# Idle matmuls behind real ones in the waits of TensorE, in the last steps of a fused attention, rational and soft-MoE kernel

## The chip, the cores and the metric

The kernel runs on one core of a Trainium2 chip. The metric is the device time of one execution in microseconds (us); the time before is the median of three runs.

## The reference

All arithmetic is float32. Three stages follow one another on 3072 tokens of width 512:

```python
# 1. chunked attention, 32 queries against 8 memory and 56 context keys
a = softmax(scale * q_c @ k_full.T); out[chunk] = a @ v_full
# 2. rational feed-forward, d_ff = 2048
h = x @ w_in
g = (a0 + a1*h + a2*h2 + a3*h3) / (1 + |b0|*|h| + |b1|*h2 + 1e-6)
x = g @ w_out
# 3. soft mixture of experts: 8 experts of 4 slots, inner width 1024
logits = x @ phi                                  # 3072 x 32
slot_input = softmax(logits, axis=0).T @ x        # 32 x 512
slot_out[e] = relu(slot_input[e] @ w1[e]) @ w2[e]
return softmax(logits, axis=1) @ slot_out
```

## The kernel before

The tokens go in 6 blocks of 512. A block has 8 steps, one for each 256 columns of w_in, so there are 48 steps (k = 0 to 47). `h_part` (L336) makes h of one step in a PSUM tile `h` of two banks (two such tiles rotate). The rational of the step runs on ScalarE and VectorE (in `run_step`, L544) and leaves g, transposed, in an SBUF tile `T`. `post` (L349) then takes that tile on TensorE: it multiplies it by `wp` (w_out times phi, L361) into the logits `lg`, and transposes it (L368) for ScalarE to copy into a `g` tile (L369). Multiplying by w_out itself is put off to the end: `soft1` (L375) to `soft3` (L413) do the running softmax of a block over its logits and add the block's slot sums, `p_tok.T @ g` (L419), to `u_acc` (L424).

The last two steps have code of their own, `last_steps` (L600). The rational of step 46 goes over whole tiles (L624, L625), that of step 47 in two halves (L628 to L630). Between them step 45 is posted (L623). After the steps `post` of 46 and 47, `soft1`, `soft2` and `soft3` of the last block follow, then the end: `u_acc` is transposed (L668), multiplied by w_out (L675) and by the softmax's denominator (L680), which gives the slot inputs; they are transposed (L683), spread by expert (L687) and go through w1 (`first`, L690) and w2 (L733, L741). The last stage multiplies by the second softmax and writes the output (L765 to L773).

w_out, w1 and w2 of the end come in pieces of 512 KB, issued by `fill` (L513) on SyncE's DMA queue (SP) into any SBUF tile that has come free. `wants` lists them in the order of use. The queue is in order, so a piece that waits for its tile holds all later pieces. The eight pieces of `fill(p_g, "g", 4, 2)` (L659) take the four `g` tiles of the last block, which `soft3` reads.

The order of TensorE outside the end is set by the framework's scheduler. Only the instructions from L714 on (and those of the start) stand in the order in which they are written. An engine takes its instructions in order.

There is already a `busy(n)` (L281) in the start of the kernel: it issues n matmuls of the identity by itself into a PSUM tile that nobody reads. They are float32, and each shows in the trace as two matmul records.

Of the kernel before, what the change touches and what calls it, by code (L numbers as in the profile page):

```python
# [43 lines left out]
def tile_chunk_attention__rational__soft_moe(  # L44
# [15 lines left out]
    PE, ACT, DVE, POOL, SP = nc.tensor, nc.scalar, nc.vector, nc.gpsimd, nc.sync  # L60

    NPAIR, P, HP, _ = qw.shape
# [4 lines left out]
    NSLOT = 32  # L67
    NE, _, EFF = w1.shape
# [3 lines left out]
    BLK = 512  # L72
    NBLK = NT // BLK
# [29 lines left out]
    ps_h = Pool(ctx.enter_context(tc.tile_pool(name="ps_h", bufs=2, space=PSUM)))  # L103
# [3 lines left out]
    def bank(shape):  # L107
        return ps_m("m", shape)
# [4 lines left out]
    ident = const("ident", [P, P])  # L113
    stack = const("stack", [P, P])
    ctab = const("ctab", [P, 8])
    wp = const("wp", [P, NF, NSLOT])
    u_acc = const("u", [P, BLK])
# [138 lines left out]
    start = ExitStack()  # L256
# [90 lines left out]
    st = {}  # L347

    def post(k, part):  # L349

        b, i = divmod(k, NSTEP)
        qd, o = divmod(i, 2)
        t_ = gt_tile[k]
        if part == 0:
            if i == 0:
                st["lg"] = ps_l("lg", [P, BLK])
            if o == 0:
                gts[b, qd] = p_g("g", [P, TT, 4 * P])
            else:
                for j in range(4):  # L360
                    PE.matmul(st["lg"][32 * j:32 * j + 32, :], lhsT=wp[:, 4 * qd + j, :],  # L361
                              rhs=gt_tile[k - 1 + j // 2][:, j % 2, :],
                              start=(qd == 0), stop=(qd == NF // 4 - 1))
        pb = bank([P, 2, 2 * P])
        for m in range(2):
            for f2 in range(2):
                tt = 2 * part + m
                PE.transpose(pb[:, m, f2 * P:f2 * P + P], t_[:, f2, tt * P:tt * P + P], ident)  # L368
        ACT.activation(gts[b, qd][:, 2 * part:2 * part + 2, 2 * P * o:2 * P * o + 2 * P], pb, AF.Copy)  # L369
        if part and o:  # L370
            del gt_tile[k - 1], gt_tile[k]
# [3 lines left out]
    def soft1(b):  # L375
        lgs = p_s2("s2", [P, BLK])
        ACT.activation(lgs, st["lg"], AF.Copy)
        lt = bank([P, BLK])
        PE.matmul(lt, lhsT=stack, rhs=lgs, start=True, stop=True)
        ct = bank([P, TT, NSLOT])  # L380
        for tt in range(TT):
            PE.matmul(ct[:, tt, :], lhsT=lgs[:, tt * P:tt * P + P], rhs=stack[:, 0:NSLOT], start=True, stop=True)
        old, neg_m = (run[:, n:n + 1] for n in ((2, 0) if b % 2 else (0, 2)))
        bm, db = p_sm("bm", [P, 1]), p_sm("db", [P, 1])
        DVE.tensor_reduce(bm, lt, AX.X, ALU.max)
        if b == 0:
            DVE.tensor_scalar(neg_m, bm, -1.0, None, ALU.mult)
        else:
            DVE.tensor_scalar(neg_m, bm, -1.0, old, ALU.mult, ALU.min)
            ACT.activation(alpha, old, AF.Exp, bias=neg_m, scale=-1.0)  # L390
        pl = p_s2("s2", [P, BLK])
        ACT.activation(pl, lt, AF.Exp, bias=neg_m, accum_out=db)
        if b == 0:
            DVE.tensor_copy(den, db)
        else:
            DVE.tensor_scalar(den, den, alpha, db, ALU.mult, ALU.add)
        cm = p_sm("cm", [P, TT])
        ce = c_all[:, b, :].rearrange("p (t s) -> p t s", t=TT)
        DVE.tensor_reduce(cm, ct, AX.X, ALU.max)
        DVE.tensor_tensor(ce, ct, cm.unsqueeze(2).to_broadcast([P, TT, NSLOT]), ALU.subtract)  # L400
        ACT.activation(ce, ce, AF.Exp)
        DVE.tensor_reduce(csum[:, b * TT:b * TT + TT], ce, AX.X, ALU.add)
        st["pl"], st["ce"] = pl, ce
# [9 lines left out]
    def soft3(b):  # L413
        ce = st.pop("ce")
        p_tok = st.pop("ptok")
        pb = bank([P, BLK])
        for tt in range(TT):
            for j in range(4):
                PE.matmul(pb[32 * j:32 * j + 32, :], lhsT=p_tok[:, tt, :], rhs=gts[b, j][:, tt, :],  # L419
                          start=(tt == 0), stop=(tt == TT - 1))  # L420
        if b == 0:
            DVE.tensor_copy(u_acc, pb)
        else:
            DVE.scalar_tensor_tensor(u_acc, u_acc, alpha, pb, ALU.mult, ALU.add)  # L424
        for j in range(4):
            del gts[b, j]
        pb = bank([P, P])
        PE.transpose(pb, ce.rearrange("p t s -> p (t s)"), ident)
        ACT.activation(c_all[:, b, :], pb, AF.Copy)

    def wp_chunk(i):
# [37 lines left out]
    def convert(what):  # L469
        kind, n = what[0], int(what[1])  # L470
        if n < NSTEP:
            for _ in {"s": split_w, "n": narrow_w_out, "w": wp_chunk, "z": wp_sum, "i": load_w_in, "o": load_w_out}[kind](n) or ():
                pass
# [55 lines left out]
    def w_out_rows(ft):  # L529
        return got["o", ft // 2][:, ft % 2, :]  # L530
# [13 lines left out]
    def run_step(kk, what):  # L544
# [52 lines left out]
        elif b == 0 and what[0] in "snwzio" and len(what) == 2:  # L597
            convert(what[0] + str(min(i + int(what[1]), NSTEP)))

    def last_steps():  # L600
        k, z = total - 2, total - 1
        for what in "a1 h0 d1 p0 p1 t a2 h1".split():
            run_step(k, what)
        hh = hs.pop(z)
        s, t, y = p_S("S", [P, 2, BLK]), p_T("T", [P, 2, BLK]), p_S("S", [P, 2, BLK])
        w = p_S("S", [P, 2, BLK])
        t_, q_, w_ = late.pop(k)
        for n in range(2):
            o = slice(n, n + 1)
            ACT.activation(s[:, o], hh[:, o], AF.Abs, scale=b0)  # L610
            ACT.activation(y[:, o], hh[:, o], AF.Square, scale=rb1)
            ACT.activation(t[:, o], hh[:, o], AF.Identity, bias=a2, scale=a3)
            DVE.scalar_tensor_tensor(s[:, o], y[:, o], QC, s[:, o], ALU.add, ALU.add)
            POOL.tensor_tensor(y[:, o], q_[:, o], w_[:, o], ALU.mult)
            DVE.tensor_tensor(t[:, o], t[:, o], hh[:, o], ALU.mult)
            DVE.scalar_tensor_tensor(t[:, o], t[:, o], a1, hh[:, o], ALU.add, ALU.mult)
        for n in range(2):
            o = slice(n, n + 1)
            ACT.activation(w[:, o], s[:, o], AF.Ln, scale=2.0 ** -LN_SHIFT)
            ACT.activation(w[:, o], w[:, o], AF.Exp, bias=ex_b, scale=-1.0)  # L620
            if n == 0:
                for part in range(2):
                    post(k - 1, part)  # L623
        DVE.scalar_tensor_tensor(t_, t_, a0, w_, ALU.add, ALU.mult)  # L624
        DVE.scalar_tensor_tensor(t_, y, 2.0, t_, ALU.subtract, ALU.mult, reverse0=True)  # L625
        for n in range(2):
            o = slice(n, n + 1)
            DVE.tensor_tensor(s[:, o], s[:, o], w[:, o], ALU.mult)  # L628
            DVE.scalar_tensor_tensor(t[:, o], t[:, o], a0, w[:, o], ALU.add, ALU.mult)
            DVE.scalar_tensor_tensor(t[:, o], s[:, o], 2.0, t[:, o], ALU.subtract, ALU.mult, reverse0=True)  # L630
        gt_tile[k], gt_tile[z] = t_, t

    for kk in range(total + 4):
        b, i = divmod(kk, NSTEP)
# [30 lines left out]

    pb = bank([P, 4, P])
    for n in range(4):
        PE.transpose(pb[:, n, :], u_acc[:, n * P:n * P + P], ident)  # L668
    ut = p_s2("s2", [P, 4, P])
    ACT.activation(ut, pb, AF.Copy)  # L670
    pb = bank([P, DM])
    for n in range(4):
        for j in range(4):
            ft = 4 * j + n
            PE.matmul(pb[32 * j:32 * j + 32, :], lhsT=ut[:, n, 32 * j:32 * j + 32],  # L675
                      rhs=w_out_rows(ft),
                      start=(n == 0), stop=(n == 3))
    fill(p_v, "v", 1, 2)
    si = p_s2("s2", [P, DM])
    ACT.activation(si, pb, AF.Copy, scale=rden)  # L680
    pb = bank([P, NC, NSLOT])
# [46 lines left out]
    for eq in range(2):  # L728
        for n in range(8 - 2 * eq):
            if eq == 0 and n in (2, 3):  # L730
                turn(1, n - 2)
            for j in range(4):
                PE.matmul(so[32 * j:32 * j + 32, :], lhsT=hts[eq][:, n, 32 * j:32 * j + 32],  # L733
                          rhs=got[("2", 4 * eq + j, n // 2)][:, n % 2, :],
                          start=(eq == 0 and n == 0), stop=False)
    W = DM // 2
    for j in range(4):
        for n in range(2):
            for w in range(2):
                g = (j + 2 * n + w) % 4  # L740
                PE.matmul(so[32 * g:32 * g + 32, W * w:W * w + W], lhsT=hts[1][:, 6 + n, 32 * j:32 * j + 32],  # L741
                          rhs=got[("2", 4 + j, 3)][:, n, W * w:W * w + W],
                          start=False, stop=(j == 3))
# [4 lines left out]
    pb = [bank([P, W]) for _ in range(2)]  # L748
# [5 lines left out]
    for b in range(NBLK):  # L754
        for half in range(2):
            ob = p_win("win", [P, 2, DM])
            if half:
                pb = [bank([P, DM]) for _ in range(2)]
            else:
                both = ps_h("h", [P, 2, DM])  # L760
                pb = [both[:, m, :] for m in range(2)]
            for m in range(2):
                g = 32 * (2 * half + m)
                for w in range(2):
                    PE.matmul(pb[m][:, W * w:W * w + W], lhsT=c_all[g:g + 32, b, :], rhs=so4[g:g + 32, w, :],  # L765
                              start=True, stop=True)
            for m in range(2):
                n = TT * b + 2 * half + m
# [66 lines left out]
```

## Time and profile before

| | |
|---|---|
| runs shown | 596.45, 598.99, 599.82 us, median 598.99 |
| the profiled execution | 599.5 us, of which the span is 597.7 us |
| busy share of the span | TensorE 91%, its weight loads 66%, VectorE 75%, ScalarE 70%, GpSimd 20% |
| mean granted clock of TensorE | 0.962 |
| DMA | 97.42 MB, mean 163 GB/s |

The span runs from the first instruction to the last. The granted clock is the part of full speed that the throttle lets TensorE have: 1.00 is 2.4 GHz, 0.50 is 1.2 GHz, and a value between them means that the level changed within the stretch. The DMA share is the mean busy share of the 16 DMA engines. An idle time with a releaser names the instruction whose end let the waiting one go.

### The profile page before, as it was taken

The page shows a single profiled execution, that of the slowest core. Times are in us where ns is not written, and L with a number is a line of the kernel's source. Part 1 is how long each engine was busy: PE and PEld are TensorE (multiplying, and loading weights), DVE is VectorE, ACT ScalarE, POOL GpSimd, SP SyncE. Part 2 cuts the span into 40 slices and gives each one's busy share as a digit, 9 for nine tenths or more (in the row PEclk, how much of TensorE's full clock was granted, in tenths as well). Part 3 has the DMA queues.
Part 4 walks back from the last instruction along what each step waited for, and adds up shares of the span by engine and source line. Part 5 has one row for each costly group of instructions (what it writes and reads, how often), then busy time and mean ns, then how long its engine had stood idle before and what let it go on. Part 6 is the DMA issues. An engine that isn't in the chain of part 4 may idle for free.

```text
span 597.7 us, 13661 instructions
## 1 busy us (share of the span) xinstructions
PE 545.7 (91%) x5944; PEld 392.3 (66%) x5944; DVE 449.3 (75%) x563; ACT 417.9 (70%) x542; POOL 120.9 (20%) x64
## 2 busy tenths in 40 slices
PE   6789699889999999999999999999999999579981
PEld 5677576667767777677776677776778577236350
DVE  3878999966987988878889698896887868721041
ACT  1589989876877878778777778687787869520131
POOL 0001221211313133131322223131322233100000
PEclk9899899798999999999999999999999999789996
DMA  8898976320220222202121032210375424969948
GB/s 353 357 325 315 370 271 236 109 104 1 107 73 19 89 71 106 72 10 98 72 107 70 3 106 72 107 38 35 107 254 169 141 77 143 390 254 383 411 167 324
DMA packets 21372, 97.42 MB, mean 163 GB/s; under 512 B 2624, under 2 KB 2752, under 8 KB 16320
## 3 DMA queue, kind: packets, MB, share of 16 engines
q1 hardware_dynamic: 20160, 92.35, 41.7%
q0 software_dynamic: 1152, 4.19, 1.7%
q8 instruction: 47, 0.77, 0.5%
q14 instruction: 13, 0.11, 0.1%
HBM read 86.05 MB, written 10.49 MB: 162 GB/s over the span
## 4 chain that ended last, share of the span: by engine, by line
PE 59%; DVE 13%; ACT 12%; DMA 8%; issue 3%; POOL 2%; SPq 0%; ACTq 0%; DVEq 0%; POOLq 0%
PE h L342 30%; PE m L368 4%; PE m L419 4%; PE lg L361 4%; ACT S L561 3%; PE m L224 3%; ACT S L562 3%; ACT g L369 2%; PE m L445 2%; DMA g<-in_moe_w_in_dram 2%; DMA g<-in_moe_w_out_dram 2%; DVE T L573 2%; DMA win<-in_moe_w_dram 2%; DVE T L574 2%; DMA T<-in_moe_w_dram 2%
## 5 line engine op out<-in xcount | busy, mean ns | idle before, releaser
L342 PE MATMUL h<-xt,win 128*128 128x512 f32 x1152 | 294.6, 404 | 7.6 <-ACT win L325 5.3
L342 PEld LDWEIGHTS h<-xt,win 128*128 128x128 f32 x1152 | 212.3, 191 | 55.2 <-ACT win L325 6.7
L539 POOL TENSOR_TENSOR S<-S,S 128x1024 f32<-128x1024 f32 x46 | 112.0, 2435 | 300.1 <-DVE S L563 288.6
L561 ACT ACTIVATE S<-h,ctab 128x1024 f32<-128x1024 f32 x47 | 52.5, 1117 | 58.1 <-PE h L342 56.4
L563 DVE SCALAR_TENSOR_TENSOR S<-S,S 128x1024 f32<-128x1024 f32 x47 | 57.5, 1223 | 45.8 <-ACT S L562 45.6
L368 PEld LDWEIGHTS m<-ident,T 128*128 128x128 f32 x384 | 44.6, 145 | 33.4 <-issue 14.5
L573 DVE TENSOR_TENSOR T<-T,h 128x1024 f32<-128x1024 f32 x47 | 57.1, 1214 | 6.7 <-ACT T L564 6.7
L368 PE MATMUL m<-ident,T 128*128 128x128 f32 x384 | 54.6, 283 | 7.9 <-DVE T L625 6.0
L574 DVE SCALAR_TENSOR_TENSOR T<-T,ctab,h 128x1024 f32<-128x1024 f32 x47 | 59.8, 1272 | 0.7
L586 DVE SCALAR_TENSOR_TENSOR T<-T,ctab,S 128x1024 f32<-128x1024 f32 x46 | 58.6, 1274 | 0.0
L587 DVE SCALAR_TENSOR_TENSOR T<-S,T 128x1024 f32<-128x1024 f32 x46 | 56.2, 1221 | 2.7 <-DVE T L586 0.5
L564 ACT ACTIVATE T<-h,ctab 128x1024 f32<-128x1024 f32 x47 | 57.5, 1223 | 0.0
L369 ACT ACTIVATE g<-m 128x512 f32<-128x512 f32 x96 | 53.4, 602 | 3.7 <-PE m L368 3.6
L579 ACT ACTIVATE S<-S,ctab 128x1024 f32<-128x1024 f32 x47 | 54.4, 1158 | 0.8
L578 ACT ACTIVATE S<-S 128x1024 f32<-128x1024 f32 x47 | 50.5, 1074 | 5.1 <-DVE S L563 3.3
L562 ACT ACTIVATE S<-h,ctab 128x1024 f32<-128x1024 f32 x47 | 52.7, 1122 | 0.5 <-DVE T L586 0.5
L361 PE MATMUL lg<-T,wp 128*32 128x512 f32 x192 | 37.2, 620 | 0.7 <-DVE T L587 0.7
L186 ACT ACTIVATE a<-a 128x512 f32<-128x512 f32 x22 | 13.7, 635 | 19.6 <-DVE a L185 19.6
L419 PE MATMUL m<-g,s 128*32 128x512 f32 x192 | 23.5, 634 | 0.4 <-ACT s L411 0.4
L333 POOL DMA_DIRECT2D wo<-win x8 | 4.7, 588 | 88.3 <-DVE win L303 68.8
L248 DVE TENSOR_TENSOR xt<-m,xt 128x512 fp32r<-128x512 f32 x24 | 16.3, 687 | 7.4 <-ACT xt L247 7.3
L247 ACT ACTIVATE xt<-m 128x512 fp32r<-128x512 f32 x24 | 14.3, 605 | 9.2 <-PE m L243 9.2
(181 smaller groups left out, 645.0 us busy)
## 6 DMA issues: line engine op xcount, KB each, us to landing
win<-in_moe_w_dram SPq DMA_DIRECT2D x32, 512.0 KB, 5.5
k<-in_kw_dram SPq DMA_DIRECT2D x11, 1024.0 KB, 6.7
v<-in_vw_dram SPq DMA_DIRECT2D x11, 1024.0 KB, 5.0
g<-in_moe_w_in_dram SPq DMA_DIRECT2D x8, 1024.0 KB, 7.4
g<-in_moe_w_out_dram SPq DMA_DIRECT2D x8, 1024.0 KB, 9.5
out_dram<-win SPq DMA_DIRECT2D x12, 512.0 KB, 6.3
q<-in_qw_dram SPq DMA_DIRECT2D x11, 512.0 KB, 4.0
wo<-win POOLq DMA_DIRECT2D x8, 512.0 KB, 6.9
```

The costliest lines, as they stand in the source:

```text
L342: PE.matmul(tile_[:, f2, :], lhsT=ww[:, c, f2 * P:f2 * P + P], rhs=xx[:, c, :], start=(n == 0), stop=(n == 3 * NC - 1))
L361: PE.matmul(st["lg"][32 * j:32 * j + 32, :], lhsT=wp[:, 4 * qd + j, :], rhs=gt_tile[k - 1 + j // 2][:, j % 2, :], start=(qd == 0), stop=(q ...
L368: PE.transpose(pb[:, m, f2 * P:f2 * P + P], t_[:, f2, tt * P:tt * P + P], ident)
L369: ACT.activation(gts[b, qd][:, 2 * part:2 * part + 2, 2 * P * o:2 * P * o + 2 * P], pb, AF.Copy)
L539: POOL.tensor_tensor(out, q, w, ALU.mult)
L561: ACT.activation(s, hh, AF.Abs, scale=b0)
L562: ACT.activation(y, hh, AF.Square, scale=rb1)
L563: DVE.scalar_tensor_tensor(s, y, QC, s, ALU.add, ALU.add)
L564: ACT.activation(t, hh, AF.Identity, bias=a2, scale=a3)
L573: DVE.tensor_tensor(t, t, hh, ALU.mult)
L574: behind[kk] = DVE.scalar_tensor_tensor(t, t, a1, hh, ALU.add, ALU.mult).ins
L586: DVE.scalar_tensor_tensor(t, t, a0, w, ALU.add, ALU.mult)
```

## The change

A new helper `keep_busy(ins, n, rhs)` places n matmuls on TensorE behind the instruction `ins`. Each multiplies the identity by the identity, or by `rhs`, into the first 128 columns of a tile `h` of PSUM that nobody reads. The tile is taken once, at the first call. In all 31 matmuls are added: 12 and 7 behind the last transpose of step 45's `post` (the 7 read `w`, ScalarE's result of step 47's first half, so they can't start before it), 5 behind the logits' turn in `soft1` of the last block, 2 behind the last transpose of `soft3`, 2 behind the transposes of `u_acc`, 3 behind the product with w_out. Nothing is removed.

```diff
@@ post
-                PE.transpose(pb[:, m, f2 * P:f2 * P + P], t_[:, f2, tt * P:tt * P + P], ident)
+                st["turn"] = PE.transpose(pb[:, m, f2 * P:f2 * P + P], t_[:, f2, tt * P:tt * P + P], ident)
@@ soft1
         for tt in range(TT):
-            PE.matmul(ct[:, tt, :], lhsT=lgs[:, tt * P:tt * P + P], rhs=stack[:, 0:NSLOT], start=True, stop=True)
+            done = PE.matmul(ct[:, tt, :], lhsT=lgs[:, tt * P:tt * P + P], rhs=stack[:, 0:NSLOT], start=True, stop=True)
+        if b == NBLK - 1:
+            keep_busy(done.ins, 5)
@@ soft3
-        PE.transpose(pb, ce.rearrange("p t s -> p (t s)"), ident)
+        done = PE.transpose(pb, ce.rearrange("p t s -> p (t s)"), ident)
+        if b == NBLK - 1:
+            keep_busy(done.ins, 2)
@@ before last_steps
+    idle = {}
+
+    def keep_busy(ins, n, rhs=None):
+        if "t" not in idle:
+            idle["t"] = ps_h("h", [P, 2, BLK])
+        with tc.issue_after(ins):
+            for _ in range(n):
+                PE.matmul(idle["t"][:, 0, 0:P], lhsT=ident, rhs=ident if rhs is None else rhs, start=True, stop=True)
+
@@ last_steps
             if n == 0:
                 for part in range(2):
                     post(k - 1, part)
+                keep_busy(st["turn"].ins, 12)
+                keep_busy(st["turn"].ins, 7, w[:, 0, 0:P])
@@ the end
-        PE.transpose(pb[:, n, :], u_acc[:, n * P:n * P + P], ident)
+        done = PE.transpose(pb[:, n, :], u_acc[:, n * P:n * P + P], ident)
+    keep_busy(done.ins, 2)
...
-            PE.matmul(pb[32 * j:32 * j + 32, :], lhsT=ut[:, n, 32 * j:32 * j + 32],
-                      rhs=w_out_rows(ft),
-                      start=(n == 0), stop=(n == 3))
+            done = PE.matmul(pb[32 * j:32 * j + 32, :], lhsT=ut[:, n, 32 * j:32 * j + 32],
+                             rhs=w_out_rows(ft),
+                             start=(n == 0), stop=(n == 3))
+    keep_busy(done.ins, 3)
```

The order of TensorE's instructions from step 45's transposes to the logits' turn, before (T_5487, T_5549 and T_5602 are the rationals of steps 45, 46 and 47):

```order
L368 MATMUL m_5625<-ident_106,T_5487 128x128 x4
L368 MATMUL m_5631<-ident_106,T_5487 128x128 x4
L368 MATMUL m_5663<-ident_106,T_5549 128x128 x4
L368 MATMUL m_5669<-ident_106,T_5549 128x128 x4
L361 MATMUL lg_5395<-T_5549,wp_109 32x512 x2
L361 MATMUL lg_5395<-T_5602,wp_109 32x512
```

and with the change, where line numbers are those of the changed file (h_5637 is the tile of the idle matmuls, S_5604 is `w`):

```order
L368 MATMUL m_5625<-ident_106,T_5487 128x128 x4
L368 MATMUL m_5631<-ident_106,T_5487 128x128 x4
L611 MATMUL h_5637<-ident_106 128x128 x12
L611 MATMUL h_5637<-S_5604,ident_106 128x128 x7
L368 MATMUL m_5683<-ident_106,T_5549 128x128 x4
L368 MATMUL m_5689<-ident_106,T_5549 128x128 x4
L361 MATMUL lg_5395<-T_5549,wp_109 32x512 x2
L361 MATMUL lg_5395<-T_5602,wp_109 32x512
```

The 19 stand between the transposes of step 45 and those of step 46, and no real instruction has changed places.

The order of TensorE's instructions around `soft3`'s last transpose and the transposes of `u_acc`, with the change:

```order
L430 MATMUL m_5762<-ident_106,call_113 128x128
L611 MATMUL h_5637<-ident_106 128x128 x2
L683 MATMUL m_5804<-ident_106,u_110 128x128 x4
L611 MATMUL h_5637<-ident_106 128x128 x2
L691 MATMUL m_5813<-x_5119,s_13_5811 32x512
```

Here, too, the idle ones are all that is new; before, L428, L668 and L675 followed one another. The 5 and the 3 stand likewise, between L382 and L409 and between L675 and L683. On the other engines and on the DMA queues the order is the same as before.

## Rows read from the trace of the kernel before

**Rows 1.** The chain that ended last: start us, us, what.

```profile
524.52 0.83 PE m L382 x8
...
526.83 0.45 PE m L409 x4
...
527.68 5.46 PE m L419 x32
...
533.17 0.76 DVE u L424
...
533.97 0.67 PE m L668 x4
...
535.37 3.69 PE m L675 x32
...
539.87 1.09 PE m L683 x8
...
562.72 10.12 DMA T<-in_moe_w_dram
```

**Rows 2.** SyncE's issues and what its queue waited for, 500 to 598 us.

```profile
533.03 3.78 SPq L526 DMA_DIRECT2D g<-in_moe_w_dram  x8
...
SPq L526 <- PE m L428: 9.4, 1, 9.4
```

**Rows 3.** Stretches: busy time by engine (instructions), granted clock, DMA share, GB/s.

```profile
514.00:515.00 1.00, 0.00 (x0) 0.00 (x0) 1.00 (x2) 1.00 (x4) 0.19 (x1) 1.00 1.01 414
515.00:516.00 1.00, 0.00 (x0) 0.00 (x0) 0.89 (x2) 0.97 (x3) 0.00 (x0) 0.60 1.03 418
...
521.00:522.00 1.00, 1.00 (x3) 0.18 (x2) 0.00 (x0) 0.00 (x0) 0.00 (x0) 0.50 1.07 426
522.00:523.00 1.00, 1.00 (x5) 0.37 (x4) 0.00 (x0) 0.26 (x1) 0.00 (x0) 0.99 1.01 401
...
528.00:529.00 1.00, 1.00 (x12) 0.26 (x8) 0.00 (x0) 0.00 (x0) 0.00 (x0) 0.93 0.90 360
529.00:530.00 1.00, 1.00 (x10) 0.24 (x6) 0.00 (x0) 0.00 (x0) 0.00 (x0) 0.50 0.16 66
...
532.00:533.00 1.00, 1.00 (x9) 0.05 (x1) 0.00 (x0) 0.00 (x0) 0.00 (x0) 0.87 0.00 0
...
534.00:535.00 1.00, 0.63 (x4) 0.39 (x4) 0.00 (x0) 0.28 (x1) 0.00 (x0) 1.00 0.95 111
...
565.00:570.00 5.00, 5.00 (x52) 1.56 (x48) 0.00 (x0) 0.00 (x0) 0.00 (x0) 1.00 1.03 409
```

**Rows 4.** TensorE in order of time: start us, us, line, tiles, count [idle before].

```profile
509.86 1.09 PE L368 MATMUL m<-ident,T 128*128 128x128 f32 x8
516.96 1.94 PE L368 MATMUL m<-ident,T 128*128 128x128 f32 x8 [6.01 <-DVE T L625]
...
521.32 1.38 PE L361 MATMUL lg<-T,wp 128*32 128x512 f32 x2
522.63 0.88 PE L368 MATMUL m<-ident,T 128*128 128x128 f32 x6
523.39 1.12 PE L379 MATMUL m<-s,stack 128*128 128x512 f32 x2
```

**Rows 5.** VectorE and ScalarE in order of time, the same stretch.

```profile
515.59 1.23 DVE L625 SCALAR_TENSOR_TENSOR T<-S,T 128x1024 f32<-128x1024 f32 x1
...
520.11 0.69 DVE L630 SCALAR_TENSOR_TENSOR T<-S,T 128x512 f32<-128x512 f32 x1
...
513.33 0.72 ACT L620 ACTIVATE S<-S,ctab 128x512 f32<-128x512 f32 x1
...
522.74 0.60 ACT L377 ACTIVATE s<-lg 128x512 f32<-128x512 f32 x1 [3.20 <-PE lg L361]
```

**Rows 6.** TensorE in order of time, 0 to 32 us: the identity matmuls of the start.

```profile
1.36 4.63 PE L284 MATMUL lg<-ident 128*128 128x128 f32 x20 [1.36 <-POOL ctab L286]
...
29.41 1.06 PE L284 MATMUL lg<-ident 128*128 128x128 f32 x8
```

## Prediction of the time after the change

> **What bounds the kernel now.** I began with the chain that ended last [rows 1]. Read from its end, it is first a DMA: the last piece of the experts' weights, issued at 562.72 and landed 10.12 us later, and everything behind it waits for that piece. So the end of the kernel is set by the stream of weights, and the next question is what holds that stream up. The DMA column answers [rows 3]: late in the stream the engines are full (share 1.03, 409 GB/s), but from 529 to 534 they are all but idle (0.16 from 529 to 530, 0.00 from 532 to 533) and full again from 534 (0.95). The queue's own waits name the cause [rows 2]: it waits 9.4 us for TensorE's L428, and at 533.03 eight pieces go out into the `g` tiles that `soft3` has just read. The stream thus starts again when L419 is done, and from there it runs full to the end. A microsecond won on TensorE before 533 is a microsecond off the end, up to the width of the gap, about 5 us.
>
> Now TensorE in that stretch. The clock column [rows 3] shows 1.00 up to 515, 0.60 from 515 to 516 and 0.50 to 522, so the level went from 2.4 to 1.2 GHz at about 515.2. Before it fell, TensorE had done nothing since step 45's transposes, which end at 510.95 [rows 4]: it waits 6.01 us for VectorE's L625. The clock is full again from 522.0. It falls a second time at 528.9 (0.93, then 0.50), behind the short waits around L409, and rises at 532.3 (0.87). L419 runs across that second fall: 5.46 us for 32 records, while L675, of the same shape and count and at full clock, takes 3.69 [rows 1].
>
> **The change part by part.** *The 31 matmuls themselves.* The nearest row is the identity matmul of the kernel's start, of the same shape: 8 records in 1.06 us, or 0.13 us a record and 0.265 us a matmul, each being two records [rows 6]. The other end is the row at 1.36 us: 20 records in 4.63 us, 0.23 us a record. I take 0.13, since the clock at 511, where the first ones start, is full. The 12 then need 3.2 us, from 510.95 to 514.1; the 7 need `w`, ready at 513.33 + 0.72 = 514.05, so they run from 514.1 to 516.0. The first real transpose starts at 516.96 behind L625 (515.59 + 1.23 = 516.82), so the 19 are hidden with 1.0 us to spare. The 5 need 1.3 us; the hole from L382's end (525.35) to L409 (526.83) is 1.48. The 2 behind L428 need 0.53 of the 0.83 us between L419's end (533.14) and L668 (533.97), and L428's own 0.14 us of pace comes out of the same hole. The 2 behind L668 (ends 534.64) have 0.73 us to L675 (535.37). The 3 behind L675 (ends 539.06) need 0.80 and the hole is 0.81 [rows 1]. So all are covered at this pace, the last with nothing to spare. I cost them at 0; the cover gone at a few tenths each, the upper end is 0.6.
>
> *Their order.* Nothing real is moved and no DMA is added or passed. The idle tile takes the PSUM buffer of step 46's h, long read. The 7 add a reader to `w`, which its refill must wait for; that refill waits for VectorE's L630 (520.80) anyway, so it costs nothing.
>
> *The last steps, if the clock stays up.* TensorE cannot run through, because VectorE is late next: the second half of step 47 comes from L630, done at 520.11 + 0.69 = 520.80, plus the 0.14 us that L625's release took, 520.94. What follows is one L361 matmul of two records. At full clock eight rounds of such records take 3.69 us (L675), 0.46 a round, so two take 0.92 and end at 521.86. ScalarE's copy L377 (0.60) and about 0.1 us of releases bring L379 to 522.55; the six transposes on TensorE (0.76 from 522.63 to 523.39 in rows 4, at full clock already) bring it to 522.62. It was 523.39 [rows 4, 5]. **Gain 0.8 us.** Of the 5 us that TensorE spent at half clock there, the rest goes into waiting for VectorE.
>
> *From L379 to L419.* This stretch ran at full clock before, so it only moves forward. *L419*: 5.46 becomes 3.69 if the second fall does not come. **Gain 1.8 us.** L424, L668, L670, L675 and L683 ran at full clock, so they gain nothing.
>
> *The sum:* 0.8 + 1.8 = 2.6 us. The eight `g` pieces go out at 530.4 instead of 533.0, well after the last earlier piece (529), and the stream moves forward by the same 2.6. From the profiled execution's 599.5 us this gives **596.9 us**. That execution is 0.5 us above the median of the three runs, so against 598.99 it is -0.35%.
>
> The bounds of the two gains: the first is at least 0 (VectorE sets it) and at most the whole 523.39 - 520.94 - 0.92 = 1.5 us, if the transposes overlapped; the second lies between 0 (the clock falls all the same) and 1.8. The two together can therefore reach 3.3 us, 596.2. Where the clock falls can differ between executions: the three runs lie 3.4 us apart, more than the gain I work out, and the fast one of 596.45 may be one that lost little here. The change would then narrow the spread as much as move the median.
>
> **The rivals.**
>
> *1. The clock falls again in spite of the idle matmuls, among the transposes.* After the 19 end at 516.0, what stands in TensorE up to 520.9 is 8 transposes, three L361 and two holes of about 1 us. For it: the transposes that started at 516.96 ran 1.94 us for 8 without the clock rising during them or for 3 us after [rows 3, 4]. Against it: the clock was at 1.00 through step 45's transposes and for 4 us more. A fall between 518 and 521 makes the last L361, the six transposes, L379 and L382 half as fast: they take 0.92 + 0.76 + 1.0 + 0.83 = 3.5 us at full clock and would lose as much again if the level were low through all of them. Much of the first low stretch of before, 515.2 to 522.0, went by in waits, so I take half, 1.7 us. That gives 598.6, and 600.4 at the worst.
>
> The Trainium skill speaks for this rival, in "TensorE: Matmul & The Clock Gate", section "Part 4: PE-mode transpose": it says that transposes do not count as TensorE being busy in the same way and that the full clock does not engage for them. The row of step 45's transposes at 1.00 doesn't decide it, since matmuls ran just ahead of them; by the rule the gain would be about 1 us, by my reading of the rows 2.6.
>
> *2. Matmuls of the identity do not hold the clock, or not these few, and everything stays as it is:* 599.5, or 599.0 at the median. For it: the operands are nearly all zeros. Against it: in the start the holes filled with L284 at the end of the stretch run at 0.13 us a record. This is also the result if the DMA stream turns out to start on something else than L419; the 9.4 us wait speaks against that.
>
> *3. The idle matmuls run long and delay the real ones.* The point from which it decides is 6.0 us / 38 records = 0.158 us a record in the first hole. At 0.23 [rows 6] the 38 last 8.8 us, to 519.8, 2.8 late. Most of that VectorE's lateness covers: transposes, L361 and the rest then bring L379 to about 523.7, 0.3 late. The 5 take 2.3 us in a hole of 1.48 (0.8 late), the 2 and 2 lose 0.3 and 0.2, the 3 lose 0.6. With L419 at half clock all the same, the sum is 2.2 us the other way: 601.7. For it: that row of the start, and that the last hole has no room to spare. Against it: the clock is full at 511.
>
> **How the numbers follow.** The forecast has 0.62, rival 1 0.16, rival 2 0.13, rival 3 0.09. The likeliest case gives 596.9 us. Its own range is 595.4 to 597.9, from the bounds of the gains and of the holes and from the half microsecond between the profiled execution and the median. To hold 8 in 10 the range takes in rivals 1 and 2 with part of the scatter: 595.2 to 599.6. A measurement of this kernel can tell about 0.5% from no change, 3.0 us, that is below 596.0 or above 602.0. The forecast lies 0.9 us short of that bound, so somewhat under half of its chance falls beyond it: faster 0.27. Slower is the worse part of rival 3, 0.05. The rest, 0.68, is the same.
>
> **What would show it.** In the profile after: a granted clock of 1.00 in every stretch from 511 to 540; the first real L368 at 516.96 still; L379 at about 522.6; L419 in about 3.7 us; the issue of the `g` pieces at about 530.4 and the last piece landing at about 570.2; idle matmuls at 0.13 us a record that end before the releaser of the next real instruction. A stretch at 0.50 after 516 would show rival 1, L419 at 5.5 us rival 2, a real matmul that starts well after its releaser rival 3. The prediction is wrong if the stream of weights ends where it did although L419 is early, or if the holes are overrun.

## The result, and the profile after

The changed kernel takes 593.38 us (median of 20 runs) where the kernel before, run beside it, took 598.94: a ratio of 0.9913, 95% interval 0.9887 to 0.9939, so 3.7 to 6.8 us. Two later measurements gave 0.9942 (0.9909 to 0.9976) and 0.9890 (0.9847 to 0.9934). The forecast was 596.9 us, with 595.2 as the lower end. The direction was right, the gain about half of what was measured first, and the time lies below the range.

These comparisons set aside runs more than 1.5% above the fastest of their kernel (the one of them with a profile, that of a2, lost its time in the first 180 us); over all runs the three means differ by 4.7, 3.1 and 3.9 us.

The profiled execution has a span of 591.7 us, 6.0 less than the one before. Its TensorE timeline (start us, us, line, tiles, count, idle before) shows where the idle matmuls, L611, came to lie:

```profile
509.04 2.84 PE L611 MATMUL h<-ident 128*128 128x128 f32 x24
512.35 1.83 PE L611 MATMUL h<-S,ident 128*128 128x128 f32 x14 [0.47 <-ACT S L633]
515.21 1.07 PE L368 MATMUL m<-ident,T 128*128 128x128 f32 x8 [1.03 <-DVE T L640]
...
519.09 1.04 PE L361 MATMUL lg<-T,wp 128*32 128x512 f32 x2 [0.57 <-DVE T L645]
...
520.83 1.13 PE L379 MATMUL m<-s,stack 128*128 128x512 f32 x2
...
522.60 1.36 PE L611 MATMUL h<-ident 128*128 128x128 f32 x10
524.26 0.43 PE L411 MATMUL m<-ident,s 32*128 32x32 f32 x4 [0.30 <-ACT s L394]
525.12 3.64 PE L421 MATMUL m<-g,s 128*32 128x512 f32 x32 [0.43 <-ACT s L413]
...
534.68 0.94 PE L611 MATMUL h<-ident 128*128 128x128 f32 x6
535.61 1.08 PE L700 MATMUL m<-stack,s 128*128 128x32 f32 x8
```

The 12 are 24 records in 2.84 us, 0.12 us a record. Each group ends before the next real instruction's releaser, but for the last: the 3 run right up to L700 (L683 before), which starts 0.05 us behind its releaser as it did before. The wait of 6.01 us [rows 4] has shrunk to 0.47 and 1.03. The eight transposes behind it take 1.07 us instead of 1.94, and L421 (L419 before) 3.64, where the same view of before has 5.34 (the 5.46 of [rows 1] is the chain's, which has 3.76 here). The stretches answer to [rows 3]: busy time by engine, granted clock, DMA share and GB/s last.

```profile
514.00:515.00 1.00, 0.18 (x2) 0.00 (x0) 1.00 (x2) 0.54 (x1) 0.00 (x0) 1.00 1.00 410
...
524.00:525.00 1.00, 0.43 (x4) 0.32 (x4) 0.76 (x6) 0.62 (x4) 0.00 (x0) 1.00 1.03 410
...
528.00:529.00 1.00, 1.00 (x11) 0.31 (x4) 0.10 (x1) 0.00 (x0) 0.00 (x0) 1.00 0.03 12
...
530.00:531.00 1.00, 0.81 (x8) 0.62 (x6) 0.00 (x0) 0.54 (x1) 0.00 (x0) 1.00 0.90 209
```

The clock is at 1.00 in each, those with waits included, and at 1.00 over the whole of 511 to 540, and the DMA engines' idle stretch is now about 2.5 us instead of 5. SyncE's queue and the chain give the rest of the way:

```profile
528.77 3.87 SPq L530 DMA_DIRECT2D g<-in_moe_w_dram  x8
```

```profile
557.99 10.14 DMA T<-in_moe_w_dram
```

The eight pieces go out 4.26 us earlier than at 533.03 [rows 2], the last piece 4.73 earlier than at 562.72 [rows 1]. Taken apart by these marks, the 6.0 us between the two profiles are: 1.75 that had been won before the last steps began (their first real transpose starts at 515.21 against 516.96), 0.81 from there to L379, 1.70 over L419, 0.4 in the stream of weights and 1.3 behind it, in the output stage. The forecast had named the second and the third of these, 0.8 and 1.8, and none of the others.

The output stage is read from its lines by source: twelve issues in 13.1 us before and 13.0 after, but the pieces land later. Before, and then with the change:

```profile
DMA to landing us min/median/max: 2.6/6.3/6.6
```

```profile
DMA to landing us min/median/max: 2.6/5.0/5.1
```

### The profile page after: what moved, and what is told of

Read it like the earlier page. It is cut to its first block, busy times and chain, and to the rows that moved or that the text cites. A ratio compares the mean times of both kernels' runs of the same rounds, so it can differ in the third digit from the quotient of the medians.

```text
span 591.7 us, 13786 instructions
## 1 busy us (share of the span) xinstructions
PE 548.6 (93%) x6006; PEld 397.0 (67%) x6006; DVE 449.0 (76%) x563; ACT 417.7 (71%) x542; POOL 120.9 (20%) x64
## 4 chain that ended last, share of the span: by engine, by line
PE 57%; DVE 14%; ACT 12%; DMA 9%; issue 3%; POOL 2%; SPq 0%; ACTq 0%; DVEq 0%; POOLq 0%
PE h L342 30%; PE m L368 4%; PE m L421 4%; PE lg L361 4%; ACT S L565 3%; DMA win<-in_moe_w_dram 3%; ACT S L566 3%; PE m L224 3%; ACT g L369 2%; DMA g<-in_moe_w_in_dram 2%; PE m L449 2%; DMA g<-in_moe_w_out_dram 2%; DVE T L577 2%; DVE T L578 2%; DMA T<-in_moe_w_dram 2%
## 5 line engine op out<-in xcount | busy, mean ns | idle before, releaser
L361 PE MATMUL lg<-T,wp 128*32 128x512 f32 x192 | 36.8, 605 | 1.3 <-DVE T L591 0.7
L421 PE MATMUL m<-g,s 128*32 128x512 f32 x192 | 21.8, 595 | 0.4 <-ACT s L413 0.4
```

## The experiments

Fourteen runs on four chips, each beside the kernel before. A profile of each shows the stages. The table has, in us: the start of L624 in the last steps; from there to L379; the length of L419; from L696's start to the use of the last piece of weights; from the first output issue to the end; and how far ahead of the end the last fetch of instructions begins (a single packet of 0.02 MB on DMA queue q8).

| kernel | idle matmuls | ratio (95%) | L624 | to L379 | L419 | stream | output | fetch |
|---|---|---|---|---|---|---|---|---|
| before | none | | 514.2 | 9.19 | 5.34 | 31.6 | 19.4 | 12 |
| b1 | none | 1.0011 (0.9988 to 1.0033) | 513.0 | 9.27 | 5.34 | 31.6 | 18.0 | 26 |
| b2 | none | one run | 510.0 | 8.38 | 5.21 | 32.0 | 19.4 | 12 |
| seven | 2, 2, 3 | 0.9998 (0.9962 to 1.0034) | 513.6 | 9.32 | 5.34 | 31.4 | 19.4 | 13 |
| five | 5 | 0.9983 (0.9953 to 1.0012) | 510.2 | 8.38 | 3.64 | 31.3 | 19.5 | 13 |
| first19 | 12, 7 | 0.9998 (0.9967 to 1.0029) | 509.1 | 8.38 | 5.18 | 31.0 | 19.3 | 15 |
| no_seven | 12, 7, 5 | 1.0002 (0.9969 to 1.0036) | 510.2 | 8.39 | 3.64 | 30.4 | 19.2 | 18 |
| no_seven_pad | 12, 7, 5; 7 early | 0.9961 (0.9931 to 0.9990) | 511.0 | 8.38 | 3.64 | 30.5 | 18.0 | 20 |
| after | all 31 | 0.9913 (0.9887 to 0.9939) | 512.4 | 8.39 | 3.64 | 31.2 | 18.0 | 20 |
| a1 | all 31 | 0.9942 (0.9909 to 0.9976) | 514.3 | 8.38 | 3.64 | 31.4 | 18.1 | 20 |
| a2 | all 31 | 0.9890 (0.9847 to 0.9934) | 517.9 | 8.38 | 3.64 | 31.3 | 18.1 | 20 |
| long24 | 24, 7, 5, 2, 2, 3 | 0.9953 (0.9920 to 0.9987) | 508.5 | 8.38 | 3.64 | 31.3 | 18.0 | 21 |
| pad33 | 33 early | 1.0039 (1.0014 to 1.0063) | 512.5 | 8.39 | 5.30 | 32.4 | 18.0 | 20 |
| early2 | all 31; 13 early | 0.9918 (0.9890 to 0.9947) | 512.5 | 8.38 | 3.64 | 30.4 | 18.0 | 21 |
| early2b | all 31; 13 early | 0.9898 (0.9863 to 0.9933) | 510.7 | 8.38 | 3.64 | 30.6 | 18.0 | 21 |
| early | all 31; 25 early | 0.9948 (0.9924 to 0.9972) | 514.6 | 8.38 | 3.64 | 31.0 | 18.0 | 24 |

**The kernel before, again (b1, b2).** No edit.

> The kernel before, once more, to learn how far its stages scatter between profiled executions. Theory A (the loss in the last steps and in L419 is of a different size in other executions, and the profiled one happened to lose little): from the first L368 of step 46 to L379 and over L419 this profile shows other times than 6.4 and 5.5 us, by 1 us or more in one of them. Theory B (these two are always about the same, and the excess over 2.6 us lies behind them, in the stream of weights and the output): L379 again 6.4 us behind that L368, L419 again 5.5 us, and from the end of L419 to the end of the span again 64.6 us. Theory C (the excess is scatter of the start): the first L368 of step 46 comes 1 to 3 us away from 516.96. Ratio 1.00 in all three.

> One more profile of the kernel before, for the scatter of its stages. If the fall of the clock is not tied to the kernel's place, L379 follows the first L368 of step 46 after anything from 5.6 to 6.5 us and L419 takes 3.6 to 5.4 us, differently from the other profiles of before (both 6.4 to 6.5 and 5.34 so far). The output stage, from its first issue to the end, takes 18.0 or 19.3 us as seen so far.

b1 repeats both losses (6.5 us from the first transpose to L379, 5.34 us for L419). b2 repeats only the second. Its L419 and three stretches:

```profile
522.68 5.21 PE L419 MATMUL m<-g,s 128*32 128x512 f32 x32 [0.43 <-ACT s L411]
```

```profile
508.00:509.00 1.00, 0.00 (x0) 0.00 (x0) 1.00 (x2) 1.00 (x2) 0.28 (x1) 0.91 1.04 389
515.00:516.00 1.00, 1.00 (x6) 0.00 (x0) 0.97 (x3) 0.34 (x1) 0.00 (x0) 0.68 1.00 406
516.00:517.00 1.00, 0.89 (x6) 0.34 (x4) 0.60 (x1) 0.00 (x0) 0.00 (x0) 1.00 1.01 406
```

Here the clock fell some 2 us after the last matmul rather than 4, and was back at 515.6, early enough for VectorE to hide everything: L379 stands 8.38 us behind L624, exactly as with the change. So the loss in the last steps depends on the execution, 0 to 0.9 us, as theory A has it; but 0.8 is near its upper end, so the profiled execution was not one that lost little. The loss over L419 was there each time. From the end of L419 to the end it is 64.7, 63.4 and 65.1 us in the three profiles of before and 62.9 to 63.2 in the three with the change: the place that theory B names is right, though the stretch scatters. What differs most is L624 itself, 510.0 to 514.2: the start of the kernel scatters by more than the change moves (theory C). The scatter lies in the first 180 us: from the first block's L419 to the last block's it is 350.3 to 352.1 us in all sixteen profiles.

**The changed kernel, again (a1, a2).** No edit.

> The changed kernel, once more. All theories: L379 5.6 us behind the first L368 of step 46, L419 in 3.6 to 3.7 us, clock 1.00 from there to the output. Theory B: from the end of L419 to the end of the span again about 62.8 us, 1.7 less than before. Theories A and C: that stretch is 63 to 64.6 us and scatters. Ratio to the kernel before: 0.9913 again by A and B, nearer to 0.9957 (2.6 us) by C.

> The changed kernel, a third time, beside the kernel with 13 more. By the stages seen so far (2.3 us up to the slot inputs, 0.3 in the stream of weights, 1.0 on average in the output stage) the gain is 3.6 us: ratio 0.994. If the first measurement's 0.9913 is the change's own doing rather than scatter of the start, it is 0.991 again.

The stages repeat to 0.1 us up to the slot inputs and in the output; L624 lies between 512.4 and 517.9. From L624 to the end of the span it is 79.3, 79.5 and 79.4 us in the three profiles, and 83.5, 82.2 and 83.0 in those of before: 3.5 us on average. The ratio moved between 0.989 and 0.994 with the start. 3.5 us would be a ratio of 0.994. Only a1's interval holds it; the other two end at 0.9939 and 0.9934. No stage behind L624 shows the 1.7 us that the first measurement has beyond the 3.5, and the profiles don't show the start earlier with the change. It may be scatter of the start; that is not shown.

**The parts (first19, five, seven, no_seven).** Each leaves some of the calls out:

```diff
@@ first19: soft1, soft3, the end
-        if b == NBLK - 1:
-            keep_busy(done.ins, 5)
...
-        if b == NBLK - 1:
-            keep_busy(done.ins, 2)
...
-    keep_busy(done.ins, 2)
...
-    keep_busy(done.ins, 3)
@@ five: last_steps, soft3, the end
-                keep_busy(st["turn"].ins, 12)
-                keep_busy(st["turn"].ins, 7, w[:, 0, 0:P])
...
-        if b == NBLK - 1:
-            keep_busy(done.ins, 2)
...
-    keep_busy(done.ins, 2)
...
-    keep_busy(done.ins, 3)
@@ no_seven: soft3, the end
-        if b == NBLK - 1:
-            keep_busy(done.ins, 2)
...
-    keep_busy(done.ins, 2)
...
-    keep_busy(done.ins, 3)
@@ seven: last_steps, soft1
-                keep_busy(st["turn"].ins, 12)
-                keep_busy(st["turn"].ins, 7, w[:, 0, 0:P])
...
-        if b == NBLK - 1:
-            keep_busy(done.ins, 5)
```

> Only the 12 and 7 idle matmuls of the first hole; the 5, 2, 2 and 3 are left out. My sum: L379 comes 5.6 us behind the first L368 of step 46 instead of 6.4, a gain of 0.8 us (ratio 0.9987); the clock then falls once more around L409, and L419 takes about 5.5 us as before, or 3.7 if the later fall no longer comes because the earlier one did not: then the gain is 2.6 (0.9957). Theory A: the gain is larger than 0.8 at the median, since executions differ in where the fall comes. Theory B: nothing changes behind L419.

> Only the 5 idle matmuls between L382 and L409. My sum: the last steps as before (6.4 us from the first L368 of step 46 to L379), L419 in 3.7 instead of 5.5 us, a gain of 1.8 us (ratio 0.9970), if the 5 alone hold the clock up; ratio 1.000 and L419 at 5.5 us if they don't. Theory A: more or less than 1.8 at the median. Theory B: nothing changes behind L419.

> The 12, 7 and 5 alone; the 2, 2 and 3 behind the last transpose of soft3, the transposes of u_acc and the product with w_out are left out. My sum: L379 5.6 us behind the first L368 of step 46, L419 in 3.6 us, the whole gain of 2.6 us (ratio 0.9957), since those three holes lie behind the fall and their work ran at full clock before. Theory D (the three small groups carry the excess, because in other executions the clock falls in one of those holes and slows the product with w_out, 3.7 us at full clock): this kernel lies 1 us or more behind the full change, at 0.997 or above, and a low stretch shows between 528 and 545 in some profile.

> The 2, 2 and 3 alone. My sum: nothing, 1.000; the last steps 6.4 us and L419 5.2 to 5.3 us in most executions. Theory D: a gain of 1 us or more at the median, 0.998 or below.

By the stages each group does its own part: with the 19 L379 stands at 8.38, but without the 5 the clock falls at L409 and L419 takes 5.18; the 5 alone bring L419 to 3.64. (That five has 8.38 too, without the 19, is the execution: as in b2, its clock fell 2 us after the last matmul.) By the ratios none of them can be told from no change. For no_seven ratio and stages disagree: its last steps and L419 alone would give about 0.9965 (2.1 us), just outside its interval of 0.9969 to 1.0036, and in its profile L624 to the end takes 79.6 us, hardly more than the change's 79.3 to 79.5. This is not explained.

Theory D expected a low stretch between 528 and 545 in a profile without the small groups. Two of the eight have one, b2 (536 to 540) and pad33 (539 to 542), and none of the eight with the small groups. It lies under L696, and the chain goes through it: in before, then in b2,

```profile
541.27 9.10 PE h L696 x80
```

```profile
536.15 10.68 PE h L696 x80
```

and these two have the longest stream of all, 32.0 and 32.4 us. So the small groups may save something there in some executions; two of eight against none of eight doesn't show that they do. But no_seven has no such stretch, and what it lacks against the change, 1.2 us, lies in the output stage (its stream was 0.8 us shorter). There the three small groups do nothing by the clock: seven and no_seven together are what led to theory E.

**The fetch (no_seven_pad, pad33).** The 7 are put into the first block, 500 us away; in pad33 the kernel before gets 33 there (14 for step 3, 7 for step 6, 12 for the last small product) and none at the end. pad33 also moves a few rows of steps 3 to 5. The edit of no_seven_pad, on top of no_seven:

```diff
+    EARLY = {(6, 0): 3, ('z', 7): 4}
     def h_part(step, tile_, f2):
...
+        for _ in range(EARLY.get((step, f2), 0)):
+            PE.matmul(tile_[:, f2, 0:P], lhsT=ident, rhs=ident, start=True, stop=True)
...
     def wp_sum(i):
...
+        for _ in range(EARLY.get(("z", i), 0)):
+            PE.matmul(pb[:, 0, :], lhsT=ident, rhs=ident[:, 0:NSLOT], start=True, stop=True)
```

> The 12, 7 and 5, without the 2, 2 and 3, and with 7 idle matmuls far away instead, in the first block (3 into step 6's h, 4 into the last small product with phi), so that TensorE's program has as many instructions as with the change. Theory E (the excess comes from a fetch of TensorE's instructions of 0.02 MB, which with the kernel before falls into the output stage and holds its last piece up by 1.3 us, and which 124 more matmul and weight-load records move ahead of that stage): from the first output issue to the end 18.0 us, with the fetch some 20 us before the end. Theory D (the small groups save the time by the clock): 19.2 us, as without the 7.

> The kernel before with 33 idle matmuls (132 records) in the first block and none at the end: 14 and 7 ahead of the h of steps 3 and 6, 12 ahead of the last small product with phi. The scheduler moves a few other instructions of steps 3 to 5 with them. Theory E: the end stays as in the kernel before up to L419 (5.2 to 5.3 us there), but the output stage takes 18.0 us instead of 19.3. Theory D: 19.3 us. What the start gains or loses by these 33 shows as the time of step 46's L624 (508 to 514 us so far).

Both have an output stage of 18.0 us. pad33 has it with L419 still at 5.30, and no_seven_pad without the small groups: theory E holds, and theory D falls for the output stage. The median landing is 5.8 us in no_seven and 5.0 in no_seven_pad. The fetch in the DMA view of before (584.7 to 585.7 us, amid the output; queue, packets, MB, share of 16 engines):

```profile
q8 instruction: 1, 0.02, 5.5%
```

The pieces show that the fetch is what delays them. In before the first four land as in b1, the fourth 6.59 us after the first issue in both. The fetch begins at 7.2 us, with the fifth on its way. The fifth's landing in before, then in b1:

```profile
DMA to landing us min/median/max: 6.6/6.6/6.6
```

```profile
DMA to landing us min/median/max: 4.9/4.9/4.9
```

Those behind it stay late, the last by 1.3 us. In first19, with the fetch at 4.0 us, the first piece to land over 1 us late is the third, and in no_seven, with the fetch at 1.0, the first. How a packet that is itself 0.9 us long in before costs 1.3 is not shown.

The table's last column shows whose fetch it is. It moves with the number of records that TensorE has more: 0 leave it 12 us ahead of the end, 20 and 28 put it at 13, 76 at 15, 96 at 18, 124 to 132 at 20, 172 to 176 at 21, 224 at 24. The size fits too: q8 brings 0.77 MB in before and TensorE has 11,888 records of matmuls and weight loads, so about 65 bytes each, and 124 records are half a packet (an estimate); no other engine has more than 563 instructions. The output stage begins 18.0 to 19.5 us ahead of the end. Wherever the fetch lies inside it (before, b2, seven, five, first19, no_seven), the stage takes 19.2 to 19.5 us; in all nine profiles in which it lies ahead, and in b1, where nothing was fetched in it and the last packet came 1.2 us behind the end, it takes 18.0 or 18.1. Why it came so late in b1 is not shown. pad33's ratio of 1.0039 says that its 33, and the rows moved with them, cost more in the first block than the 1.3 us that they save.

**An overrun (long24).** 24 for the 12:

```diff
-                keep_busy(st["turn"].ins, 12)
+                keep_busy(st["turn"].ins, 24)
```

> The change with 24 instead of 12 idle matmuls in the first hole: the price of an overrun (rival 3). At 0.24 us a matmul, as the profile after shows, the 12 more take 2.9 us where 1.0 was spare, so the first L368 of step 46 starts about 2.0 us behind its releaser instead of at once. VectorE's lateness hides part of that: the last L361 waited 0.6 us for it, so L379 should come 1.3 to 1.5 us later than with the change, and the time goes up by as much (about +0.0024 of ratio against the change). If the idle matmuls gave way to real ones, nothing would change.

The first real transpose started 3.52 us behind L624's start instead of 2.76, only 0.76 late, and L379 came at 8.38 as before: VectorE hid all of it. The forecast of 1.3 us was too high, since a late start lets the L361 of both tiles run closer together (six records in 1.22 us, 1.95 with the change). Twice the number overruns the first hole and costs nothing here.

**More of it (early2, early, early2b).** All 31, and 5 and 8 early (early2, early2b) or 12, 5 and 8 (early), by the `EARLY` table above.

> The whole change and 13 idle matmuls more in the first block (5 ahead of step 6's h, 8 ahead of the last small product with phi), where the clock fell at 109 and at 132 us in 6 of 10 profiles. If those falls cost what the profiles without them suggest (step 46's L624 at 508.5 to 510.2 us without, 512.4 to 514.3 with them), L624 comes at 510 us or before in every execution, and the time is 591 to 592 us, about 2 us below the change. If VectorE or ScalarE sets those steps anyway, the time is that of the change. The output stage takes 18.0 us by theory E.

> As the kernel with 13 more, and 12 more again ahead of step 3's h, in the hole of 3.7 us at 62 us behind which the clock falls in nearly every profile (64 to 72 us). The scheduler moves a few other instructions of steps 3 to 5 with them. If that fall is on the path of the first block: 1 to 2 us less again, 590 us. If DMA or VectorE sets that part, no difference to the kernel with 13.

> The kernel with 13 more idle matmuls in the first block, beside the change on the same chip. If the 13 gain anything, it lies 1 to 2 us below the change (0.991); if its earlier 0.9918 was scatter, both are the same.

The aim failed: the clock still falls at 130 us in early2 and at 131 in early2b. TensorE of early2 there, and two stretches:

```profile
130.45 1.87 PE L455 MATMUL m<-u,S 128*128 128x32 f32 x8
```

```profile
129.00:130.00 1.00, 1.00 (x11) 1.00 (x10) 1.00 (x2) 1.00 (x2) 0.00 (x0) 1.00 0.03 8
...
131.00:132.00 1.00, 1.00 (x7) 1.00 (x7) 1.00 (x2) 0.00 (x0) 1.00 (x1) 0.50 0.00 0
```

TensorE shows as busy from 129 on (0.46 from 128 to 129, behind a wait of 0.54 us), with matmuls of 32 columns behind full weight loads, and the clock goes to half all the same; in early2b it shows 1.00 in each stretch from 128 to 131 and the clock falls at 131.4. L624 isn't at 510 or before either (512.5 and 510.7). The kernel's two ratios, 0.9918 and 0.9898, lie among the change's three; beside a2 they can't be told apart. In early the falls at 64 and 130 are gone, and it gains nothing (0.9948), so that part is not on the path, or what the moved rows cost hides it; which of the two was not tried. The falls in the first block do go with the scatter: L624 stands at 508.5 to 510.2 us in the five profiles without those at 109 and 130, at 510.7 to 512.5 in the four with the later one and at 512.4 to 517.9 in the six with both; early, with none and at 514.6, is the exception. (Of the ten profiles that the expectation of early2 counts, five had those falls, not six.) No version was shown to beat the change.

## Why the prediction was wrong

- *What bounds the kernel*: right. The stream started when L419 was done in all sixteen profiles, 0.01 to 0.02 us behind it, and from there to L696 it is 8.25 us in each, so what was won before it was kept. Behind that the margin is small: in no_seven, no_seven_pad, early2 and early2b, with streams of 30.4 to 30.6 us, TensorE no longer waited for the last piece.
- *The 31 matmuls*: hidden, as forecast, at 0.12 us a record for the 12 where 0.13 was taken; the last hole had nothing to spare, and needed nothing.
- *"No DMA is added or passed", costed at 0*: **this step failed.** The matmuls are also instructions, 124 records with their weight loads, and TensorE's code comes in by DMA. They moved a fetch of 0.02 MB from within the output stage, where it lay in before and b2 (not in b1), to ahead of it; the stage takes 18.0 to 18.1 us instead of 19.2 to 19.5. The edit was priced as time on TensorE alone.
- *The last steps, 0.8*: 0.81 in the profiled pair, 0.9, 0 and 0.9 in b1, b2 and seven and 0 in five and pad33, whose last steps are also those of before: 0.4 on average. The mechanism was right; the profiled execution was taken for the typical one.
- *L419, 1.8*: 1.70, and 1.57 in b2. Right.
- *The stream moves forward by the same*: nearly; 31.6 to 32.0 us before and 31.2 to 31.4 after, 0.3 to 0.4 us more than forecast, over a scatter of 30.4 to 32.4 in all profiles. Part of b2's 32.0 is L696 at half clock; for the rest no cause is shown.
- The sum of the stages by these averages is 0.4 + 1.7 + 0.3 + 1.0 = 3.4 us, against 2.6 (from L624 to the end the profiles gave 3.5); the fetch is the 1.0. The measured 3.7 to 6.8 us has more than that, and the rest stays open.
- *The rivals*: the first, a fall among the transposes, didn't come in any of the ten profiles with the 19: in the profile after, eight transposes, three L361 and waits of 1.03 and 0.57 us behind them passed at 1.00. The Trainium skill ("TensorE: Matmul & The Clock Gate", "Part 4: PE-mode transpose") has it that the full clock does not engage for transposes. Here, with the idle matmuls just ahead, the eight took 1.07 us at 1.00, so this trace does not agree; what transposes alone would do is not shown. The second and third didn't come; in long24 the 31 in the first hole do delay a real transpose, by 0.76 us, at no cost.
- *The range*: 595.2 allowed for the bounds of the two gains and a part of the scatter, but the start alone moves L624 between 508 and 518. The fetch priced at the 1.3 us of the profiled pair would have put the forecast at 595.6 and the lower end at 593.9; the measured 593.4 lies below even that, so the fetch is not all of the miss.

## What to carry to other kernels

Where a wait of some microseconds is followed by TensorE work on the path, try matmuls that nobody reads, queued behind the last real one and, for a long wait, hung in part on an input that becomes ready inside it. Here they delayed no real instruction, and the clock stayed at 1.00. Price an added instruction twice, as time and as code: look in the DMA view for the fetches of instructions and for what they lie under. When a program's start scatters by more than the change is worth, compare the stages from a common mark rather than the total.

## What was not expected of the hardware

- One fetch of 0.02 MB of instructions under a full stream of output held its last piece up by 1.3 us (landing 6.3 us after issue at the median instead of 5.0), beginning with the piece that was on its way when the fetch began.
- Under matmuls of 32 columns behind full weight loads, with two transposes between them, TensorE showed as busy, 1.00 in each stretch from 128 to 131 us of early2b, and the granted clock fell to 0.50 at 131.4.
- In the same wait of 6.0 us the clock fell 4.2 to 4.5 us after the last matmul in three executions (before, b1, seven) and 2.0 to 2.2 us after it in three others (b2, five, pad33); the first three lost 0.8 to 0.9 us in the work behind it, the others nothing.
